# Two attention blocks on one core: K and P transposed in tiles of 64 rows, K no longer by DMA transpose

## The chip, the core and the metric

The kernel runs on one core of one Trainium2 chip. The metric is the device time of one execution in microseconds (us); the median of the runs is quoted. The core has five engines with instruction queues of their own: TensorE (PE, with its weight loads listed apart as PEld), VectorE (DVE), ScalarE (ACT), GpSimd (POOL) and SyncE (SP), which here only starts loads. Transfers go through 16 DMA engines. Matmul results go to PSUM, eight banks of 128 rows by 512 f32 (or 1024 bf16) columns; everything else lies in SBUF.

## The reference

Two independent attention blocks, A and B, with the same shapes; the two results stand side by side in the output.

```python
# x (16, 64, 640), k_cache and v_cache (16, 32, 512, 128), wq (640, 4096), wo (4096, 640), all bf16
q = (x @ wq).reshape(B, Sq, 32, 128).transpose(0, 2, 1, 3)
scores = einsum("bhqd,bhkd->bhqk", q, k_cache) * (128 ** -0.5)
p = softmax(scores, axis=-1)
o = einsum("bhqk,bhkd->bhqd", p, v_cache)
return o.transpose(0, 2, 1, 3).reshape(B, Sq, 4096) @ wo
```

K and V of both blocks are 268 MB, and each byte is used once.

## The kernel before

**Tiling.** Two batches of 64 queries fill the 128 rows: a batch pair `bp`, with batches `j` = 0 and 1. A *step* `g` is one head of a batch pair, a *macro* `m` is two heads, a *chunk* `c` four, and a *group* the 16 heads of one half of the heads. There are 512 steps, 256 macros, 128 chunks and 32 groups: two blocks, two halves of the heads (a block and a half make a *pass*, which keeps its weights), eight batch pairs.

**One macro in order.** K comes from memory with keys on the rows and must be turned so that the head's 128 features are on the rows. KX (`em_KX`, L451) does this on PE: for each batch, eight transposes of 128x128 (L457) put the keys of two heads into bank 7, and KE (L466, DVE) copies the 1024 columns to `ktp_ring`. QP2 (L475, PE) computes q of two heads, ten 128-column matmuls, QE2 (L484, ACT) scales and copies it. SM (L496, PE) makes the scores of one head: two matmuls of 512 columns, one for each batch, on the two column halves of the array (`tile_position=(0, 64 * j)`), so that batch `j` lands in rows 64j to 64j+63 of one of four score banks. MX (L505, DVE) takes the row maxima, EX (L511, ACT) the exponentials and row sums, RC2 (L517, DVE) the reciprocals, NM (L525, POOL) scales P and reorders its columns. TR2 (L534, PE) transposes P of both heads, eight transposes of 128x128 into bank 6; TE2 (L541, DVE) or TA2 (L546, ACT) copies the 1024 columns to `pT_ring`. PV2 (L558, PE) multiplies with V, 16 matmuls of 64 columns with V as the stationary operand; OE2 (L566, ACT) copies it out. OP2 (L574, PE) multiplies with the first 512 columns of wo and adds over the 16 heads of a group in bank 0. Once per group OX (L584, PE) does the same for the last 128 columns, in score bank 0; OVP and OXP (ACT) keep the sums of the first half of the heads, OVF and OXF (DVE) add the second half, and ST (L613) stores from ACT's queue.

**K by DMA.** In the eleven groups of `TGROUPS` (L20) the K of batch 1 is loaded already transposed: LDKT (L651) is one DMA transpose of 2 MB per group into `kd_sb`. There KX and KE run for batch 0 alone, and SM reads `kd_sb`. The x operand comes by DMA transposes too (LDX, L644).

**What orders the work.** `build_plan` writes each engine's program from a template (`PE_T`, `ACT_T`, `DVE_T`, `POOL_T`, L33 to L43): a list of kind, macro offset, which of two heads, and a time in a period of 6.7 us that covers two macros. Each engine executes its list strictly in that order; semaphores make it wait for what it reads and for buffers to come free (`Op.reads`, `Op.writes`). Loads (L195 to L263) all go through SP's queue in one order: a planner sorts them by when they are due, not before the buffer that they fill is free by its own estimate (`SLOT_NS`, `DMA_NS`). K has four slots of a chunk (two DMAs of 512 KB, one for each batch), V five; the last chunk is loaded in halves (`TAIL_SPLIT`).

The transposes of K, and the banks before:

```python
            for t8 in range(8):
                ins = e.transpose(kt_ps[:, t8, :], kn_ring[:, c % NKB, j, hp, t8, :], ident[:, :])
...
        S_BANK0 = 2
        OUT_BANK, QO_BANK, PT_BANK, KT_BANK = 0, 1, 6, 7
```

Of the kernel before, what the change touches and what calls it, by code (L numbers as in the profile page):

```python
# [14 lines left out]
class Cfg:  # L15
    G = 4
    HH = 16
    NKB = 4
    NW = 6
    TGROUPS = (4, 6, 11, 13, 15, 19, 21, 23, 27, 29, 31)  # L20
    TLEAD = 1.0
    NVB = 5
    XLEAD = 1.5
    NQ = 3
    NKT = 5
    NP = 4
    NPN = 4
    NT = 2
    NO = 9
    NR = 8  # L30
    NS = 4
    PERIOD = 6.7
    PE_T = (("SM", 0, 0, 0.0), ("SM", 0, 1, 0.21), ("SM", 1, 0, 0.43), ("SM", 1, 1, 0.64), ("KX", 2, 1, 0.98),  # L33
            ("PV2", -3, 0, 1.43), ("TR2", -2, 0, 1.9), ("OP2", -4, 0, 2.35), ("KX", 3, 1, 2.78), ("QP2", 3, 0, 3.23),
            ("OP2", -3, 0, 3.79), ("OX", -3, 0, 4.2), ("KX", 3, 0, 4.22), ("PV2", -2, 0, 4.67), ("TR2", -1, 0, 5.14),
            ("KX", 4, 0, 5.59), ("QP2", 4, 0, 6.04))
    ACT_T = (("EX", 0, 0, 1.13), ("OE2", -3, 0, 2.1), ("EX", 0, 1, 2.49), ("TA2", -2, 0, 3.15), ("QE2", 3, 0, 4.0),
             ("EX", 1, 0, 4.4), ("OXP", -3, 0, 5.2), ("OE2", -2, 0, 5.34), ("EX", 1, 1, 5.73), ("OVP", -3, 0, 6.4),
             ("QE2", 4, 0, 6.65), ("ST", -3, 0, 6.68))
    DVE_T = (("MX", 0, 0, 0.44), ("MX", 0, 1, 1.06), ("RC2", -1, 0, 1.66), ("KE", 2, 1, 1.68), ("MX", 1, 0, 2.3),  # L40
             ("TE2", -2, 0, 2.6), ("RC2", 0, 0, 3.3), ("KE", 3, 1, 3.43), ("MX", 1, 1, 4.1), ("KE", 3, 0, 4.87),
             ("OXF", -3, 0, 5.3), ("OVF", -3, 0, 5.5), ("TE2", -1, 0, 5.79), ("KE", 4, 0, 6.4))
    POOL_T = (("NM", -1, 0, 1.95), ("NM", -1, 1, 2.8), ("NM", 0, 0, 4.2), ("NM", 0, 1, 5.05))  # L43
    TAIL_SPLIT = 2
    SLOT_NS = 3400.0
    DMA_NS = dict(LDK=3100.0, LDKT=9600.0, LDV=3100.0, LDWQ=3900.0, LDWO=4300.0, LDX=700.0)


class Op:
# [3 lines left out]
    def __init__(self, eng, kind, idx, reads=(), writes=(), dur=0.0, ts=None, aux=None):  # L53
# [12 lines left out]
        self.dma = kind in ("LDK", "LDKT", "LDV", "LDX", "LDWQ", "LDWO", "ST")  # L66


def build_plan(dims, cfg):
# [3 lines left out]
    assert H % HH == 0 and HH % G == 0 and G % 2 == 0 and cfg.NR % 2 == 0 and B % 2 == 0  # L73
# [9 lines left out]
    HG = HH // G  # L83
    MPG = SPB // 2
    MPP = NBP * MPG
    MPC = G // 2
    KT = dims["KT"]

    def step_info(g):
# [8 lines left out]
    def by_dma(m, j=1):  # L98
        return j == 1 and m // MPG in cfg.TGROUPS

# [657 lines left out]
```

## Time and profile before

| | |
|---|---|
| median of 3 runs | 898.91 us (897.99 to 900.96) |
| profiled execution, its own time | 900.23 us |
| its span in the profile | 898.5 us |
| granted TensorE clock | 0.996 of full speed |
| busy: PE, PEld, DVE, ACT, POOL | 857.5, 691.1, 746.6, 628.0, 413.8 us |
| moved by DMA | 296.81 MB, mean 330 GB/s |

The page divides the span among engines and among 40 slices, follows the chain of work that ended last back from the end (here 78% PE and 9% DMA), and lists groups of instructions by line with their number, the mean duration of one and the idle time before them. A matmul's duration includes the way through the array, and consecutive ones overlap: 128 columns show 219 to 221 ns each but follow one another every 56 ns. So the cost of PE's work is read from the distance between starts, which the timeline and the single records give, and not from durations. The same holds, with smaller differences, for DVE and ACT. DMA shares over 1 mean that packets of several transfers lie in a DMA engine at once.

The costliest groups before are, in us of busy time: POOL's scaling of P 413.1 (512 instructions of 843 ns), EX 350.1 (512 of 684), MX 337.3 (512 of 680), KE 290.0 (424 of 684), the transposes of K 263.6 (3392 matmuls), QP2 187.8 (2560), PV2 162.0 (4096), the transposes of P 156.4 (2048). A K or V load of 512 KB takes 9.3 to 9.9 us from issue to landing, a DMA transpose of K 17.9.

### The profile page before, as it was taken

The page shows a single profiled execution, that of the slowest core. Times are in us where ns is not written, and L with a number is a line of the kernel's source. Part 1 is how long each engine was busy: PE and PEld are TensorE (multiplying, and loading weights), DVE is VectorE, ACT ScalarE, POOL GpSimd, SP SyncE. Part 2 cuts the span into 40 slices and gives each one's busy share as a digit, 9 for nine tenths or more (in the row PEclk, how much of TensorE's full clock was granted, in tenths as well). Part 3 has the DMA queues.
Part 4 walks back from the last instruction along what each step waited for, and adds up shares of the span by engine and source line. Part 5 has one row for each costly group of instructions (what it writes and reads, how often), then busy time and mean ns, then how long its engine had stood idle before and what let it go on. Part 6 is the DMA issues. An engine that isn't in the chain of part 4 may idle for free.

```text
span 898.5 us, 33204 instructions
## 1 busy us (share of the span) xinstructions
PE 857.5 (95%) x14016; PEld 691.1 (77%) x14144; DVE 746.6 (83%) x1398; ACT 628.0 (70%) x1651; POOL 413.8 (46%) x518
## 2 busy tenths in 40 slices
PE   4999989999999999999998998999999999999997
PEld 3777777878888877878786787778778777787875
DVE  2888878888888888888887887888888798888896
ACT  1776766777777777767676776777777676776774
POOL 0544444445444454544444444445454444545453
PEclk9999999999999999999999999999999999999999
DMA  9999999999999999999999999999999999999992
GB/s 304 336 340 365 318 272 365 295 361 365 363 366 368 286 361 322 319 369 270 364 361 368 367 260 365 309 324 366 294 363 363 367 370 284 367 286 365 315 333 77
DMA packets 315172, 296.81 MB, mean 330 GB/s; under 512 B 109200, under 2 KB 260752, under 8 KB 315024
## 3 DMA queue, kind: packets, MB, share of 16 engines
q1 hardware_dynamic: 312720, 292.06, 106.3%
q10 hardware_dynamic: 2304, 2.62, 0.9%
q8 instruction: 111, 1.82, 0.9%
q14 instruction: 37, 0.30, 0.1%
HBM read 266.34 MB, written 2.62 MB: 299 GB/s over the span
## 4 chain that ended last, share of the span: by engine, by line
PE 78%; DMA 9%; SPq 7%; DVE 3%; issue 1%; ACT 1%; DVEq 0%; ACTq 0%
PE ps L457 20%; PE ps L475 14%; PE ps L496 12%; PE ps L558 11%; PE ps L534 10%; PE ps L574 9%; DMA kn_ring<-in_B_k_cache_dram 5%; DMA kn_ring<-in_A_k_cache_dram 4%; SPq L651 3%; PE ps L584 3%; SPq L644 2%; DVE ktp_ring L466 1%; SPq L664 1%; DMA wq_sb<-in_A_wq_dram 1%; DVE negmax L505 1%
## 5 line engine op out<-in xcount | busy, mean ns | idle before, releaser
L525 POOL TENSOR_SCALAR pn_ring<-p_ring,recip 128x512 bf16<-128x512 bf16 x512 | 413.1, 843 | 476.1 <-DVE recip L517 475.7
L511 ACT ACTIVATE p_ring<-ps,negmax 128x512 bf16<-128x512 f32 x512 | 350.1, 684 | 100.0 <-DVE negmax L505 100.0
L466 DVE COPY ktp_ring<-ps 128x1024 bf16<-128x1024 bf16 x424 | 290.0, 684 | 82.1 <-PE ps L457 67.2
L505 DVE TENSOR_REDUCE negmax<-ps 128x1 f32<-128x512 f32 x512 | 337.3, 680 | 15.2 <-PE ps L496 4.9
L457 PEld LDWEIGHTS ps<-ident,kn_ring 128*128 128x128 bf16 x3392 | 205.3, 98 | 108.5 <-issue 46.5
L457 PE MATMUL ps<-ident,kn_ring 128*128 128x128 bf16 x3392 | 263.6, 221 | 21.1 <-DMA kn_ring<-in_A_k_cache_dram 11.8
L475 PE MATMUL ps<-xT_sb,wq_sb 128*128 128x128 bf16 x2560 | 187.8, 221 | 1.3 <-DMA wq_sb<-in_A_wq_dram 0.6
L558 PE MATMUL ps<-pT_ring,v_ring 128*128 128x64 bf16 x4096 | 162.0, 193 | 8.6 <-DMA v_ring<-in_B_v_cache_dram 3.1
L475 PEld LDWEIGHTS ps<-xT_sb,wq_sb 128*128 128x128 bf16 x2560 | 154.4, 99 | 16.9 <-ACT oT_ring L566 15.8
L558 PEld LDWEIGHTS ps<-pT_ring,v_ring 128*128 128x128 bf16 x4096 | 141.9, 98 | 28.5 <-issue 26.5
L484 ACT ACTIVATE qT_ring<-ps 128x256 bf16<-128x256 f32 x256 | 98.3, 384 | 86.1 <-PE ps L475 86.0
L534 PE MATMUL ps<-ident,pn_ring 128*128 128x128 bf16 x2048 | 156.4, 219 | 0.0
L566 ACT ACTIVATE oT_ring<-ps 128x256 bf16<-128x256 f32 x256 | 97.6, 381 | 75.3 <-PE ps L558 68.1
L541 DVE COPY pT_ring<-ps 128x1024 bf16<-128x1024 bf16 x174 | 119.5, 687 | 35.5 <-PE ps L534 35.5
L496 PE MATMUL ps<-ktp_ring,qT_ring 128*64 128x512 bf16 x848 | 137.3, 391 | 0.0
L574 PE MATMUL ps<-wo_sb,oT_ring 128*128 128x512 bf16 x384 | 124.5, 379 | 6.8
L534 PEld LDWEIGHTS ps<-ident,pn_ring 128*128 128x128 bf16 x2048 | 118.5, 98 | 0.0
L511 ACT ACTIVATION_READ_ACCUMULATOR p_ring<-ps,negmax 128x1 f32 x512 | 103.1, 201 | 0.0
L546 ACT ACTIVATE pT_ring<-ps 128x1024 bf16<-128x1024 bf16 x82 | 84.0, 1024 | 0.0
L496 PEld LDWEIGHTS ps<-ktp_ring,qT_ring 128*64 128x64 bf16 x848 | 47.1, 110 | 41.0 <-issue 2.1
L517 DVE RECIPROCAL recip<-rowsum 128x2 f32<-128x2 f32 x256 | 40.9, 160 | 14.7 <-ACT p_ring L511 14.6
L496 PE MATMUL ps<-kd_sb,qT_ring 128*64 128x512 bf16 x176 | 47.0, 390 | 0.0
(15 smaller groups left out, 152.0 us busy)
## 6 DMA issues: line engine op xcount, KB each, us to landing
v_ring<-in_A_v_cache_dram SPq DMA_DIRECT2D x128, 512.0 KB, 9.9
v_ring<-in_B_v_cache_dram SPq DMA_DIRECT2D x126, 512.0 KB, 9.8
kn_ring<-in_A_k_cache_dram SPq DMA_DIRECT2D x108, 512.0 KB, 9.4
kn_ring<-in_B_k_cache_dram SPq DMA_DIRECT2D x103, 512.0 KB, 9.3
wq_sb<-in_A_wq_dram SPq DMA_DIRECT2D x8, 640.0 KB, 9.9
wo_sb<-in_A_wo_dram SPq DMA_DIRECT2D x8, 640.0 KB, 10.7
wq_sb<-in_B_wq_dram SPq DMA_DIRECT2D x8, 640.0 KB, 9.7
wo_sb<-in_B_wo_dram SPq DMA_DIRECT2D x8, 640.0 KB, 10.3
```

The costliest lines, as they stand in the source:

```text
L457: ins = e.transpose(kt_ps[:, t8, :], kn_ring[:, c % NKB, j, hp, t8, :], ident[:, :])
L466: ins = e.tensor_copy(dst, src)
L475: ins = e.matmul(q_ps[:, sub * 128:(sub + 1) * 128], wq_sb[:, wslot(ps_, hh // G), kt, (hh % G) * DH:(hh % G + 1) * DH], xT_sb[:, kt, bp * ...
L484: ins = e.activation(qT_ring[:, m % NQ].rearrange("p s q -> p (s q)"), q_ps, ACTF.Copy, scale=scale)
L496: ins = e.matmul(s_bank(2 * m + sub)[64 * j:64 * j + 64, :], qT_ring[:, m % NQ, sub, 64 * j:64 * j + 64], kt, start=True, stop=True, tile_ ...
L505: ins = e.reduce_max(negmax[:, r:r + 1], s_bank(g), axis=AX.X, negate=True)
L511: ins = e.activation(p_ring[:, g % NP, :], s_bank(g), ACTF.Exp, bias=negmax[:, r:r + 1], scale=1.0, accum_out=rowsum[:, r:r + 1])
L525: ins = e.tensor_scalar(dst, src, recip[:, r:r + 1], 1.0, ALU.mult, ALU.mult)
L534: ins = e.transpose(pt_ps[:, sub, t, :], pn_ring[:, g % NPN, t * 128:(t + 1) * 128], ident[:, :])
L541: ins = e.tensor_copy(pT_ring[:, m % NT].rearrange("p s t q -> p (s t q)"), pt_ps_flat)
L558: ins = e.matmul(o_ps[:, col:col + 64], v_ring[:, c % NVB, j, gi, t, :], pT_ring[:, m % NT, sub, t, 64 * j:64 * j + 64], start=(t == 0), s ...
L574: ins = e.matmul(out_ps, oT_ring[:, m % NO, sub, :], wo_sb[:, wslot(ps_, hh // G), hh % G, 0:N0], start=(hh == 0), stop=(hh == SPB - 1))
```

## The change

KX and TR no longer run 128x128 transposes. Each is split into two tiles of 64 rows (`row_transpose`): tile r takes rows 64r to 64r+63 of the operand, uses the row half r of the array (`tile_position=(64 * r, 0)`) and writes 64 columns to a bank of its own. K now has banks 4 and 5, P banks 6 and 7, and the score banks go from four to two. For K the two halves are the two heads of a macro, for P the two batches.

KX handles a whole macro, both batches at once, 32 transposes, and KE copies 2048 columns in one instruction; there are 256 KE where there were 424. TR has 16 transposes per macro, and one of two P copies runs on DVE, the other on ACT. `TGROUPS`, `kd_sb` and LDKT are gone: all of K comes through KX, loaded in 512 KB DMAs that hold two heads of both batches (ten slots). QP4, PV4 and their copies QE4 and OE4 handle a chunk at a time, 512 columns in one bank that q and o share. In the template each half of a turn has one visit for scores, one for KX and TR together, and one for the rest. OX writes to P's first bank instead of score bank 0, all 16 heads at once for the last group too. The last chunk is not split.

The core of the diff (templates, resources, loads, banks, transposes, K's and V's DMAs; the four-head forms of QP, QE, PV and OE differ from the old ones in their loops alone):

```diff
 class Cfg:
     G = 4
     HH = 16
-    NKB = 4
+    NKU = 10
+    NVB = 5
     NW = 6
-    TGROUPS = (4, 6, 11, 13, 15, 19, 21, 23, 27, 29, 31)
-    TLEAD = 1.0
-    NVB = 5
-    XLEAD = 1.5
-    NQ = 3
-    NKT = 5
+    XLEAD = 2.0
+    NQ = 4
+    NKT = 3
     NP = 4
     NPN = 4
-    NT = 2
-    NO = 9
+    NT = 4
+    NO = 10
     NR = 8
-    NS = 4
-    PERIOD = 6.7
-    PE_T = (("SM", 0, 0, 0.0), ("SM", 0, 1, 0.21), ("SM", 1, 0, 0.43), ("SM", 1, 1, 0.64), ("KX", 2, 1, 0.98),
-            ("PV2", -3, 0, 1.43), ("TR2", -2, 0, 1.9), ("OP2", -4, 0, 2.35), ("KX", 3, 1, 2.78), ("QP2", 3, 0, 3.23),
-            ("OP2", -3, 0, 3.79), ("OX", -3, 0, 4.2), ("KX", 3, 0, 4.22), ("PV2", -2, 0, 4.67), ("TR2", -1, 0, 5.14),
-            ("KX", 4, 0, 5.59), ("QP2", 4, 0, 6.04))
-    ACT_T = (("EX", 0, 0, 1.13), ("OE2", -3, 0, 2.1), ("EX", 0, 1, 2.49), ("TA2", -2, 0, 3.15), ("QE2", 3, 0, 4.0),
-             ("EX", 1, 0, 4.4), ("OXP", -3, 0, 5.2), ("OE2", -2, 0, 5.34), ("EX", 1, 1, 5.73), ("OVP", -3, 0, 6.4),
-             ("QE2", 4, 0, 6.65), ("ST", -3, 0, 6.68))
-    DVE_T = (("MX", 0, 0, 0.44), ("MX", 0, 1, 1.06), ("RC2", -1, 0, 1.66), ("KE", 2, 1, 1.68), ("MX", 1, 0, 2.3),
-             ("TE2", -2, 0, 2.6), ("RC2", 0, 0, 3.3), ("KE", 3, 1, 3.43), ("MX", 1, 1, 4.1), ("KE", 3, 0, 4.87),
-             ("OXF", -3, 0, 5.3), ("OVF", -3, 0, 5.5), ("TE2", -1, 0, 5.79), ("KE", 4, 0, 6.4))
-    POOL_T = (("NM", -1, 0, 1.95), ("NM", -1, 1, 2.8), ("NM", 0, 0, 4.2), ("NM", 0, 1, 5.05))
-    TAIL_SPLIT = 2
-    SLOT_NS = 3400.0
-    DMA_NS = dict(LDK=3100.0, LDKT=9600.0, LDV=3100.0, LDWQ=3900.0, LDWO=4300.0, LDX=700.0)
+    NS = 2
+    PERIOD = 5.85
+    PE_T = (("SM", 0, 0, 0.0), ("SM", 0, 1, 0.21), ("KX", 2, 0, 0.54), ("TR", -2, 0, 1.0), ("PV4", -2, 0, 1.35),
+            ("OP", -5, 0, 2.28), ("OX", -5, 0, 2.71), ("SM", 1, 0, 2.82), ("SM", 1, 1, 3.03), ("KX", 3, 0, 3.36),
+            ("TR", -1, 0, 3.82), ("QP4", 2, 0, 4.16), ("OP", -4, 0, 5.28))
+    ACT_T = (("EX", 0, 0, 1.15), ("EX", 0, 1, 1.81), ("OE4", -2, 0, 2.52), ("OVP", -5, 0, 3.0), ("OXP", -5, 0, 3.4),
+             ("EX", 1, 0, 3.97), ("EX", 1, 1, 4.63), ("ST", -5, 0, 4.7), ("TE", -1, 0, 5.3), ("QE4", 2, 0, 6.45))
+    DVE_T = (("MX", 0, 0, 0.44), ("MX", 0, 1, 1.06), ("TE", -2, 0, 1.68, True), ("KE", 2, 0, 1.7),
+             ("TE", -2, 0, 2.85, False), ("OVF", -5, 0, 3.2),
+             ("OXF", -5, 0, 3.4), ("MX", 1, 0, 3.46), ("RC2", 0, 0, 4.08), ("MX", 1, 1, 4.22), ("KE", 3, 0, 4.85),
+             ("RC2", 1, 0, 6.0))
+    POOL_T = (("NM", 0, 0, 4.35), ("NM", 0, 1, 5.2), ("NM", 1, 0, 6.2), ("NM", 1, 1, 7.05))
+    SLOT_NS = 3000.0
+    DMA_NS = dict(LDK=1300.0, LDV=1500.0, LDWQ=1950.0, LDWO=2150.0, LDX=700.0)
...
+        if kind == "KX":
+            return mk(eng, "KX", m, [("kn", m % cfg.NKU), ("ident",)], [("KTB",)], ts)
+        if kind == "KE":
+            return mk(eng, "KE", m, [], [("KTB",), ("ktp", m % cfg.NKT)], ts)
+        if kind == "SM":
+            return mk(eng, "SM", (m, sub), [("qT", m % cfg.NQ), ("ktp", m % cfg.NKT)], [("SB", g % cfg.NS)], ts)
...
+            return mk(eng, "OX", m, [("oT", i % cfg.NO) for i in range(m + 1 - MPG, m + 1)]
+                      + [("wo", wslot(ps_, i)) for i in range(HG)], [("PTB",)], ts)
+        home = {"V": ("OUTB",), "X": ("PTB",)}.get(kind[1])
...
+    by_chunk = ("QP4", "QE4", "PV4", "OE4")
...
+        for k in range(-6, NCHUNK + 6):
+            late = (2 * k - 5) % MPG == MPG - 1
+            for kind, off, sub, t, *when in tmpl:
+                if when and when[0] != late:
+                    continue
...
+        for j in range(2):
+            m = 2 * c + j
+            ready = at["KX", m - cfg.NKU, 0] if m >= cfg.NKU else NEG
+            first = at["KX", m, 0]
+            add(ready, first, first, 2, "LDK", m, [("kn", m % cfg.NKU)], m, cfg.DMA_NS["LDK"])
+            ready = at["PV4", c - cfg.NVB, 0] if c >= cfg.NVB else NEG
+            first = at["PV4", c, 0]
+            add(ready, first, first, 2.5, "LDV", (c, j), [("v", c % cfg.NVB, j)], (c, j), cfg.DMA_NS["LDV"])
     pending = sorted(loads, key=lambda e: (e[1], e[2]))
...
-        kn_ring = sb("kn_ring", [128, NKB, 2, G // 2, 8, DH], BF16)
+        kn_ring = sb("kn_ring", [128, NKU, 2, 8, DH], BF16)
         v_ring = sb("v_ring", [128, NVB, 2, G, 4, DH], BF16)
-        kd_sb = sb("kd_sb", [128, 8, HH * 64], BF16)
-        ktp_ring = sb("ktp_ring", [128, NKT, 2, SK], BF16)
+        ktp_ring = sb("ktp_ring", [128, NKT, 2, 2, SK], BF16)
...
-        S_BANK0 = 2
-        OUT_BANK, QO_BANK, PT_BANK, KT_BANK = 0, 1, 6, 7
+        OUT_BANK, QO_BANK, S_BANK0, KT_BANK, PT_BANK = 0, 1, 2, 4, 6
         out_ps = ps[:, OUT_BANK, :]
-        pt_ps_flat = ps[:, PT_BANK, :].bitcast(BF16)
-        pt_ps = pt_ps_flat.rearrange("p (s t q) -> p s t q", s=2, t=4)
-        q_ps = ps[:, QO_BANK, 0:256]
-        o_ps = ps[:, QO_BANK, 256:512]
-        kt_ps_flat = ps[:, KT_BANK, :].bitcast(BF16)
-        kt_ps = kt_ps_flat.rearrange("p (t s) -> p t s", t=8)
+        qo_ps = ps[:, QO_BANK, :]
+        kt_ps = [ps[:, KT_BANK + r, :].bitcast(BF16) for r in range(2)]
+        kt_ps_both = ps[:, KT_BANK:KT_BANK + 2, :].bitcast(BF16)
+        pt_ps = [ps[:, PT_BANK + r, :].bitcast(BF16) for r in range(2)]
+        pt_ps_both = ps[:, PT_BANK:PT_BANK + 2, 0:256].bitcast(BF16)
+        ox_ps = ps[:, PT_BANK, 0:N1]
 
         def s_bank(g):
             return ps[:, S_BANK0 + g % NS, :]
 
-        ox_ps = ps[:, S_BANK0, 0:N1]
+        def row_transpose(e, banks, r, i, src):
+            half = slice(64 * r, 64 * r + 64)
+            return e.transpose(banks[r][:, 64 * i:64 * i + 64], src, ident[half, half], tile_position=(64 * r, 0))
 
         def em_KX(e, op):
-            m, j = op.idx
-            g0 = 2 * m
-            c, hp = g0 // G, (g0 % G) // 2
             first = last = None
-            for t8 in range(8):
-                ins = e.transpose(kt_ps[:, t8, :], kn_ring[:, c % NKB, j, hp, t8, :], ident[:, :])
-                first = first or ins
-                last = ins
+            for j in range(2):
+                for t in range(8):
+                    for r in range(2):
+                        ins = row_transpose(e, kt_ps, r, 8 * j + t,
+                                            kn_ring[64 * r:64 * r + 64, op.idx % NKU, j, t, :])
+                        first = first or ins
+                        last = ins
             return first, last
 
         def em_KE(e, op):
-            m, j = op.idx
-            src = kt_ps_flat.rearrange("p (t hs pp) -> p t hs pp", t=8, hs=2)
-            dst = ktp_ring[:, kslot(m, j)].rearrange("p hs (t pp) -> p t hs pp", t=8)
-            ins = e.tensor_copy(dst, src)
-            return ins, ins
-
-        def em_QP2(e, op):
-            m = op.idx
+            ins = e.tensor_copy(ktp_ring[:, op.idx % NKT].rearrange("d r j s -> d r (j s)"), kt_ps_both)
+            return ins, ins
+
...
-        def em_TR2(e, op):
+        def em_TR(e, op):
             m = op.idx
             first = last = None
             for sub in range(2):
-                g = 2 * m + sub
                 for t in range(4):
-                    ins = e.transpose(pt_ps[:, sub, t, :], pn_ring[:, g % NPN, t * 128:(t + 1) * 128], ident[:, :])
-                    first = first or ins
-                    last = ins
-            return first, last
-
-        def em_TE2(e, op):
-            m = op.idx
-            ins = e.tensor_copy(pT_ring[:, m % NT].rearrange("p s t q -> p (s t q)"), pt_ps_flat)
-            return ins, ins
-
-        def em_TA2(e, op):
-            m = op.idx
-            ins = e.activation(pT_ring[:, m % NT].rearrange("p s t q -> p (s t q)"), pt_ps_flat, ACTF.Copy)
-            return ins, ins
-
-        def em_PV2(e, op):
-            m = op.idx
-            first = last = None
-            for sub in range(2):
-                g = 2 * m + sub
-                c, gi = g // G, g % G
-                for j in range(2):
-                    for t in range(4):
-                        col = sub * 128 + 64 * j
-                        ins = e.matmul(o_ps[:, col:col + 64], v_ring[:, c % NVB, j, gi, t, :],
-                                       pT_ring[:, m % NT, sub, t, 64 * j:64 * j + 64], start=(t == 0), stop=(t == 3))
+                    for r in range(2):
+                        ins = row_transpose(e, pt_ps, r, 4 * sub + t,
+                                            pn_ring[64 * r:64 * r + 64, (2 * m + sub) % NPN, t * 128:(t + 1) * 128])
                         first = first or ins
                         last = ins
             return first, last
 
-        def em_OE2(e, op):
-            m = op.idx
-            ins = e.activation(oT_ring[:, m % NO].rearrange("p s q -> p (s q)"), o_ps, ACTF.Copy)
-            return ins, ins
-
-        def em_OP2(e, op):
+        def em_TE(e, op):
+            dst = pT_ring[:, op.idx % NT].rearrange("p j s t q -> p j (s t q)")
+            if op.eng == "act":
+                ins = e.activation(dst, pt_ps_both, ACTF.Copy)
+            else:
+                ins = e.tensor_copy(dst, pt_ps_both)
+            return ins, ins
+
...
-        def em_LDKT(e, op):
-            blk, bp, grp, ps_, _ = step_info(2 * op.aux[0])
-            h0 = (ps_ % NHALF) * HH
-            src = blocks[blk][1][2 * bp + 1, h0:h0 + HH].rearrange("h (p t) d -> (h p) (t d)", t=8)
-            ins = e.dma_start_transpose(kd_sb[:, :, :], src)
-            return ins, ins
-
-        def em_LDKV(e, op):
-            c, j, hlo, hhi, _piece = op.aux
+        def em_LDK(e, op):
+            blk, bp, grp, ps_, hh = step_info(2 * op.idx)
+            h0 = (ps_ % NHALF) * HH + hh
+            src = blocks[blk][1][2 * bp:2 * bp + 2, h0:h0 + 2].rearrange("j hs (p t) d -> (hs p) j (t d)", t=8)
+            ins = e.dma_start(kn_ring[:, op.idx % NKU].rearrange("p j t d -> p j (t d)"), src)
+            return ins, ins
+
+        def em_LDV(e, op):
+            c, j = op.aux
             blk, bp, grp, ps_, hh0 = step_info(c * G)
             h0 = (ps_ % NHALF) * HH + hh0
-            if op.kind == "LDV":
-                src = blocks[blk][2][2 * bp + j, h0 + hlo:h0 + hhi].rearrange("g (p t) d -> p g t d", p=128)
-                ins = e.dma_start(v_ring[:, c % NVB, j, hlo:hhi], src)
-            else:
-                src = blocks[blk][1][2 * bp + j, h0 + hlo:h0 + hhi].rearrange("(hp hs) (p t) d -> (hs p) hp t d",
-                                                                              hs=2, t=8)
-                ins = e.dma_start(kn_ring[:, c % NKB, j, hlo // 2:hhi // 2], src)
-            return ins, ins
-
```

## The prediction

> **What bounds the kernel now.** I call a *turn* one pass of the planner's templates: two macros, four heads of one batch pair; there are 128. The page's second part shows the DMA row at 9 tenths in all slices but the last, and PE busy 95%, so either may set the end. I read the busy time by stretches first, cut where the trace shows DMA transposes being issued (columns: stretch, its length, busy us of PE, PEld, DVE, ACT, POOL, granted clock, DMA share, GB/s).
>
> ```profile
> 180.00:295.00 115.00, 114.11 (x1897) 93.01 (x1913) 99.93 (x187) 86.42 (x225) 55.58 (x70) 1.00 1.08 365
> ...
> 643.00:735.00 92.00, 89.76 (x1490) 72.72 (x1501) 78.94 (x149) 66.88 (x177) 42.58 (x53) 1.00 1.08 366
> ...
> 880.00:882.00 2.00, 1.83 (x28) 1.27 (x26) 2.00 (x6) 1.77 (x6) 1.26 (x2) 1.00 0.26 81
> 882.00:898.50 16.50, 11.16 (x179) 7.76 (x180) 8.23 (x16) 6.64 (x19) 6.73 (x9) 0.99 0.03 11
> ```
>
> ```profile
> 112.00:128.00 16.00, 15.84 (x269) 13.05 (x271) 13.60 (x27) 12.32 (x32) 7.12 (x9) 1.00 1.18 239
> ...
> 349.00:368.00 19.00, 18.84 (x309) 15.20 (x310) 16.82 (x34) 13.54 (x36) 8.51 (x11) 1.00 1.20 260
> ...
> 840.00:860.00 20.00, 19.84 (x343) 16.85 (x344) 17.55 (x35) 14.93 (x38) 9.69 (x12) 1.00 1.18 277
> ```
>
> Without a transpose in flight the DMA moves 363 to 366 GB/s whatever the engines do; with one, 239 to 277 at a *higher* DMA share (1.18 to 1.20 against 1.08). The loads end at about 881 us and 17 us of computing follow. The account closes: 296.81 MB at 365 GB/s are 813 us; the eleven stretches with K by DMA last 206 us and move 54.4 MB, worth 149 us, so they lose 57; the first 5 us (91 GB/s) lose 4; the remaining x transposes about 7. Sum 881. **So the memory queue sets the end, and 57 us of it are the price of K by DMA.**
>
> PE is close behind. The chain of waits, in order of time (start, length, line), gives a turn:
>
> ```profile
> 187.99 0.56 PE ps L475 x10
> ...
> 193.83 0.56 PE ps L475 x10
> ...
> 206.42 0.56 PE ps L475 x10
> ...
> 213.15 0.56 PE ps L475 x10
> ```
>
> 5.84 us where half of K comes by DMA, 6.73 where it does not. With 16 OX matmuls (0.90 us in the same chain) per group: 44 x 5.84 + 84 x 6.73 + 32 x 0.90 = 851 us, plus 8.6 before the first transpose and some 12 of tail: 872. The memory floor and PE lie 26 us apart; a change must lower both.
>
> **The terms on PE.** The timeline, start to start, prices PE's visits (columns: start, length, what).
>
> ```profile
> 61.73 1.05 PE L496 MATMUL ps<-ktp_ring,qT_ring 128*64 128x512 bf16 x8
> ...
> 62.72 0.62 PE L457 MATMUL ps<-ident,kn_ring 128*128 128x128 bf16 x8
> ...
> 63.17 0.63 PE L558 MATMUL ps<-pT_ring,v_ring 128*128 128x64 bf16 x16
> ...
> 63.64 0.61 PE L534 MATMUL ps<-ident,pn_ring 128*128 128x128 bf16 x8
> ...
> 65.17 0.69 DVE L466 COPY ktp_ring<-ps 128x1024 bf16<-128x1024 bf16 x1
> ...
> 65.78 0.68 DVE L505 TENSOR_REDUCE negmax<-ps 128x1 f32<-128x512 f32 x1
> ```
>
> Eight 128-column transposes take 0.45 us (56 ns each); sixteen 64-column PV matmuls, each with its own 128x128 weight load, 0.47 (29 ns each); eight score matmuls 0.99. In the records the last score pair is followed by the next mode 312 ns later where the pair itself streams 216, and QP to scores is 149 ns where QP to QP is 56: a change of array mode costs about 95 ns.
>
> The unknown is a 64-row transpose: no row tile runs in this trace. Its 64 columns cost at most a PV matmul, 29 ns, if the two row halves go one after the other, and 14.5 if they go side by side. The nearest row is the score pair, two column halves of the array:
>
> ```profile
> 883.63 0.40 PE L496 MATMUL ps<-ktp_ring,qT_ring 128*64 128x512 bf16 x1
> 883.64 0.40 PE L496 MATMUL ps<-kd_sb,qT_ring 128*64 128x512 bf16 x1
> ...
> 883.87 0.38 PE L496 MATMUL ps<-ktp_ring,qT_ring 128*64 128x512 bf16 x1
> 883.88 0.38 PE L496 MATMUL ps<-kd_sb,qT_ring 128*64 128x512 bf16 x1
> ```
>
> Halves start 4 to 10 ns apart and a pair costs one. Weight loads can follow that fast too: 5% of the gaps between L457's are 15 ns or less. The new emitter gives the halves a bank each, so I take 29 ns a pair. Below that I see no reason to go; the upper end, 58 a pair, is the first rival.
>
> The new turn: transposes of K, 2 x 16 pairs = 0.94 (was 4 x 0.45 = 1.80); of P, 2 x 8 pairs = 0.47 (was 0.90); PV 32 x 29 = 0.94, QP 20 x 56 = 1.12, OP 4 x 216 = 0.86, all as before; scores in two visits, 2 x (0.24 + 0.31) = 1.10; four further changes of mode at 95 ns = 0.38. Sum 5.81; the old turn has 0.12 over its own sum, so 5.93, and OX adds 0.90 / 4: **6.15 us, 128 turns = 788**, with start and tail about 809.
>
> **The other engines per turn.** DVE: a 1024-column copy is 0.61 start to start, as a 512-column f32 reduce is. A 2048-column copy lies between that plus the second half's 0.53 (0.69 less some 0.15 of fixed cost), 1.14, and two old copies, 1.22; I take 1.15. If the wider form fell to the reduce's pace (512 elements in 0.61) it would be 2.4, but same type and source at 1024 columns exclude that. So 4 x 0.61 + 2 x 1.15 + 0.61 + 2 x 0.17 = 5.7, with OVF and OXF 5.8. ACT: 4 x 0.66 + a P copy 0.94 + two 512-column copies at 0.49 (0.28 + 256 more columns) = 4.6. POOL: 4 x 0.79 = 3.2. Two score banks in place of four put SM(1) behind EX(0): MX 1.3 and EX 1.4 after SM(0) stand inside the 2.8 us that the template leaves. OX moves from a score bank to P's pair, where the template copies P ahead of it in that turn; its 0.9 us are in the sum. DVE's in-order queue has KE ahead of MX, so a late K stops maxima too; PE then waits for both at once, which costs nothing while K is what is late.
>
> **The memory queue.** Same bytes, K now in 2 KB pieces. 297 MB at 365: 813. About 13,000 more instructions (PE's 28,160 become some 42,000) are 0.8 MB: 2. First 5 us: 4. The six x transposes stay: between 7 (their 2.6 of 25.7 transposed MB, of 64 us lost) and 12; I take 9. **Loads end near 828, or 6.4 us a turn; PE with 6.15 fits under it.** No ring starves it: ten K and five V slots (five turns) cover 9.9 us from issue to landing.
>
> By the Trainium skill (DMA: Bandwidth & Descriptors, "Where 436 GB/s comes from") a core has about 358 GB/s of its memory. The trace grants 365; by the page this term would be 829 in place of 813.
>
> Tail: the last V loads are due three chunks behind the last K, 6 x 1.43 = 8.6 us. From the last K to the end, by rows: transposes and copy 1.9, two macros of scores, maxima and exponentials to 6, two POOL steps to 8, TR and copy 9.6, PV 10.7, OE4, OP and 16 OX 13.3, final adds 14.4, store 2.4: 17 us, or 8 after the last load. Before had 17, with PE behind, though it loaded its last chunk in halves; unsplit, the last load lands 0.7 later. I take 11.
>
> Span 828 + 11 = 839; the profiled execution lay 1.7 above its span (900.23 against 898.5) and the median 1.3 below that: **840 us**.
>
> **Rivals.**
> 1. *Row halves one after the other* (slower). Each K macro costs 0.94, each P macro 0.47: the turn grows by 1.41 to 7.56, 968 us of turns, 988 in all. It decides from a pair of about 44 ns, where 128 turns and 21 us reach 898. Against it: the score pairs. For it: no row tile in the trace, and 64-column matmuls never stand closer than 27 ns within one tile. By the Trainium skill (TensorE: Matmul & The Clock Gate, "Wait — 56ns, not 53.3ns?") matmuls never start less than about 25 ns apart however few columns; held between tiles, that gives some 50 ns a pair, 7.16 x 128 + 21 = 937 us. The trace's 4 ns between score halves speaks against it.
> 2. *Hand-offs keep PE above the queue's pace.* Six modes a turn, one transpose bank pair, one QO bank for both projections and PV, DVE at 5.8 of 6.4. With 0.5 us of waits a turn, 6.65 x 128 + 21 = 872. For it: DVE's margin is now 10%, was 17%. Against it: the old turn lost only 0.12 to such waits.
> 3. *K in its new shape is read slower*: two batches 4 MB apart per partition. At V's rate by packet time (1 KB in 50.9 ns against 2 KB in 89.7), 134 MB lose some 45 us: 885.
>
> **How the numbers follow.** Forecast 0.70, own range 831 (tail 8, x 7, no price for instructions) to 864 (356 GB/s, the slowest clean stretch, 860 to 880 us). Rival 2: 0.10, 864 to 885. Rival 3: 0.04. Rival 1: 0.14, 905 to 988. Gains that cancel, within 0.3% (what a measurement of this kernel tells from none): 0.02. Faster 0.84. The range 831 to 880 leaves out rival 1, most of rival 3 and edges: about 2 in 10.
>
> **What the profile after would show.** Right: no stretch under 330 GB/s but at x; sixteen K pairs in about 0.47 us with halves under 10 ns apart; PE waits on kn_ring spread over the run; loads ending near 828. Wrong: 32 transposes in 0.9 us, the DMA row under 9, and no kn_ring waits (rival 1); DVE the releaser of L457's and L496's idle time (rival 2); clean stretches under 350 GB/s (rival 3).

## The result, and the profile after

The changed kernel takes **996.36 us** (median of 4 runs, 994.34 to 1007.66) against 898.76 us for the kernel before on the same chip: a ratio of 1.1107, 95% interval 1.1022 to 1.1192 (ratios here are estimated over all executions, so they are not exactly the quotient of the medians). It is 11% slower where 840 us and a gain were forecast. The profiled execution took 996.13 us, with a span of 994.4. Its page, cut to the lines that answer to the first reading of the profile before (busy time, slices, one DMA queue, the chain):

```profile
span 994.4 us, 47021 instructions
PE 841.7 (85%) x20992; PEld 587.6 (59%) x20992; DVE 725.2 (73%) x1184; ACT 638.9 (64%) x1441; POOL 416.4 (42%) x518
...
PEclk9888999989999999999999899999999989999999
DMA  9999998879859999989967999899993999898850
GB/s 284 364 336 366 340 344 289 292 263 348 307 194 367 361 298 309 300 300 319 320 246 255 367 318 337 282 307 308 337 363 128 369 369 333 279 302 285 286 188 15
...
q8 instruction: 166, 2.72, 1.1%
...
PE 82%; issue 13%; SPq 2%; DMA 1%; DVE 1%; ACT 1%; POOL 0%; ACTq 0%
```

PE has less to do than before (841.7 us busy, was 857.5), the DMA moves less in the mean (299 GB/s, was 330), and neither is full any more. The chain holds 13% "issue", time in which the engine waited for nothing that the profile shows; before it was 1%. The same two rows of the page before:

```profile
q8 instruction: 111, 1.82, 0.9%
...
PE 78%; DMA 9%; SPq 7%; DVE 3%; issue 1%; ACT 1%; DVEq 0%; ACTq 0%
```

The waits of PE say where (columns: line, releaser, us in total, times, longest):

```profile
PE ps L401 <- issue: 54.9, 42, 3.2
PE ps L498 <- issue: 39.3, 26, 3.1
PE ps L423 <- issue: 30.1, 17, 2.7
...
PE ps L514 <- issue: 4.9, 5, 2.4
```

Of the releasers that the prediction watched for, kn_ring has no row for PE at all and DVE one of 1.3 us. PE stops in every kind of its work alike, up to 3 us at a time, with no semaphore behind it. One such stop in the timeline, matmuls first, weight loads second (start, length, what, idle before):

```profile
200.27 1.29 PE L423 MATMUL ps<-xT_sb,wq_sb 128*128 128x128 bf16 x20
...
202.48 0.64 PE L401 MATMUL ps<-ident,kn_ring 64*128 64x64 bf16 x32
202.96 0.40 PE L401 MATMUL ps<-ident,pn_ring 64*128 64x64 bf16 x16
203.29 1.11 PE L498 MATMUL ps<-pT_ring,v_ring 128*128 128x64 bf16 x32
...
206.79 1.01 PE L514 MATMUL ps<-wo_sb,oT_ring 128*128 128x512 bf16 x2 [2.40 <-issue]
...
210.13 2.31 PE L423 MATMUL ps<-xT_sb,wq_sb 128*128 128x128 bf16 x20
```

```profile
204.20 0.10 PEld L514 LDWEIGHTS ps<-wo_sb,oT_ring 128*128 128x128 bf16 x1
206.80 0.11 PEld L514 LDWEIGHTS ps<-wo_sb,oT_ring 128*128 128x128 bf16 x1 [2.50 <-issue]
```

Three things stand in these lines. The transposes are as fast as forecast: 32 of K from 202.48 to 202.96, 16 of P to 203.29. Then the weight load of an OP starts at 204.20 and its own matmul only at 206.79. And after the pause the 20 matmuls of L423 take 2.31 us, where they took 1.29 at 200.27: the granted clock has dropped to half, in windows of 3.4 us, 97 us in all (9 us before).

**What PE waits for.** The page lists a DMA queue with the kind "instruction": 166 transfers of 16 KB, 2.72 MB. PE's records (20,992 weight loads, 20,992 matmuls and 655 of its sequencer, such as semaphore waits) number 42,639. That is 64 bytes a record, 256 records a transfer, and 166.6 such blocks (a *block* from here on is one of these, not an attention block). The singled-out stop fits: a transfer of this queue starts at 204.30, lands at 205.27, and PE goes on 1.5 us later. All records can be counted by their place in the program, modulo 256. A stop is here a start that lies more than 0.45 us behind the start before it; matmuls that the trace lacks are filled in from their weight loads; "one place" is record 193 of 256, where 91 of the kernel after's stops lie, give or take four records.

```
                      records  blocks  stops over   us in   at one place  us at     mean
                                of 256   0.45 us     all       mod 256   that place
before                 28,615   111.8       30       38.6           1       0.8     0.84
after                  42,639   166.6      142      192.4          92     150.9     1.64
```

The stops elsewhere are the start and the end of the run, waits for data, and ordinary steps stretched by the half clock. PE stops where one block of 256 instructions ends and the next has not landed; it goes on 1.27 to 1.58 us (in 9 of 10, median 1.41) after the landing. How long after the *preceding* block end the next block lands depends on how busy the DMA engines are in between (kernel after, means; the share counts packet time up to the landing, and over 1 is a backlog):

```
DMA share between         under 0.3  0.3-0.6  0.6-0.8  0.8-0.95  0.95-1.05  over 1.05
block lands after, us          2.2      2.9       3.3       4.1        4.0        5.0
mean stop, us                 0.00     0.24      0.11      0.87       0.99       1.29
blocks                          12        5        13        32         44         59
```

Two stretches of the kernel after show the same in the busy times (stretch, its length, PE, PEld, DVE, ACT, POOL, clock, DMA share, GB/s): 504 matmuls in 25 us beside full loads, 625 beside a third of them.

```profile
300.00:325.00 25.00, 20.79 (x504) 14.36 (x505) 17.34 (x28) 14.68 (x32) 9.29 (x12) 0.93 1.07 369
750.00:775.00 25.00, 22.32 (x625) 15.86 (x623) 21.64 (x35) 18.67 (x44) 11.80 (x15) 1.00 0.41 133
```

So beside full data loads PE gets one block per **6.5 us, 39 instructions a microsecond**: the mean distance of the block ends in the 59 intervals of the last column, 5.0 to the landing and some 1.4 more; its own pace without stops (below) is 4.8 us a block. Between any two block ends exactly one transfer lands (165 of 165 in the kernel after): the supply runs one block ahead and no further, so a slack stretch saves nothing for a dense one.

### The profile page after: what moved, and what is told of

Its sections match the earlier page's. It is cut to its first block, busy times and chain, and to the rows that moved or that the text cites. A ratio compares the mean times of both kernels' runs of the same rounds, so it can differ in the third digit from the quotient of the medians.

```text
span 994.4 us, 47021 instructions
## 1 busy us (share of the span) xinstructions
PE 841.7 (85%) x20992; PEld 587.6 (59%) x20992; DVE 725.2 (73%) x1184; ACT 638.9 (64%) x1441; POOL 416.4 (42%) x518
## 3 DMA queue, kind: packets, MB, share of 16 engines
q8 instruction: 166, 2.72, 1.1%
## 4 chain that ended last, share of the span: by engine, by line
PE 82%; issue 13%; SPq 2%; DMA 1%; DVE 1%; ACT 1%; POOL 0%; ACTq 0%
PE ps L401 22%; PE ps L423 17%; PE ps L439 15%; PE ps L498 14%; PE ps L514 12%; PE ps L524 3%; DMA v_ring<-in_A_v_cache_dram 1%; SPq L591 1%; SPq L584 0%; DVE negmax L448 0%; SPq L570 0%; ACT p_ring L454 0%; ACT pT_ring L486 0%; DVE ktp_ring L415 0%; DVE pT_ring L488 0%
## 5 line engine op out<-in xcount | busy, mean ns | idle before, releaser
L415 DVE COPY ktp_ring<-ps 128x2048 bf16<-128x2048 bf16 x256 | 311.3, 1216 | 30.1 <-PE ps L401 29.5
L401 PEld LDWEIGHTS ps<-ident,kn_ring 64*128 64x128 bf16 x8192 | 140.6, 97 | 145.2 <-issue 142.1
L423 PE MATMUL ps<-xT_sb,wq_sb 128*128 128x128 bf16 x2560 | 182.3, 230 | 38.2 <-issue 30.1
L401 PE MATMUL ps<-ident,kn_ring 64*128 64x64 bf16 x8192 | 174.9, 193 | 31.3 <-issue 29.7
L423 PEld LDWEIGHTS ps<-xT_sb,wq_sb 128*128 128x128 bf16 x2560 | 156.6, 103 | 47.2 <-issue 32.6
L514 PE MATMUL ps<-wo_sb,oT_ring 128*128 128x512 bf16 x512 | 162.3, 400 | 5.2 <-issue 4.9
L486 ACT ACTIVATE pT_ring<-ps 128x1024 bf16<-128x1024 bf16 x128 | 130.6, 1021 | 17.9 <-PE ps L401 17.8
L401 PE MATMUL ps<-ident,pn_ring 64*128 64x64 bf16 x4096 | 108.0, 193 | 29.7 <-issue 25.2
L506 ACT ACTIVATE oT_ring<-ps 128x512 bf16<-128x512 f32 x128 | 76.2, 595 | 63.3 <-PE ps L498 63.0
L432 ACT ACTIVATE qT_ring<-ps 128x512 bf16<-128x512 f32 x128 | 76.9, 601 | 48.2 <-PE ps L423 48.1
L401 PEld LDWEIGHTS ps<-ident,pn_ring 64*128 64x128 bf16 x4096 | 81.4, 97 | 34.0 <-issue 30.6
L514 PEld LDWEIGHTS ps<-wo_sb,oT_ring 128*128 128x128 bf16 x512 | 37.8, 102 | 7.2 <-issue 6.0
```

The costliest lines, as they stand in the source:

```text
L401: return e.transpose(banks[r][:, 64 * i:64 * i + 64], src, ident[half, half], tile_position=(64 * r, 0))
L415: ins = e.tensor_copy(ktp_ring[:, op.idx % NKT].rearrange("d r j s -> d r (j s)"), kt_ps_both)
L423: ins = e.matmul(qo_ps[:, i * 128:(i + 1) * 128], wq_sb[:, wslot(ps_, hh // G), kt, i * DH:(i + 1) * DH], xT_sb[:, kt, bp * 128:(bp + 1) * ...
L432: ins = e.activation(qT_ring[:, s0:s0 + 2].rearrange("p m s q -> p (m s q)"), qo_ps, ACTF.Copy, scale=scale)
L486: ins = e.activation(dst, pt_ps_both, ACTF.Copy)
L514: ins = e.matmul(out_ps, oT_ring[:, m % NO, sub, :], wo_sb[:, wslot(ps_, hh // G), hh % G, 0:N0], start=(hh == 0), stop=(hh == SPB - 1))
```

## The experiments

Theory 1: PE lacks instructions, because the change raised their number by half and the data loads delay their blocks. Theory 2: row tiles, with six changes of array mode a turn, cost this time as such. Theory 3: hand-offs (two score banks, one pair of transpose banks) hold PE up.

**1. The kernel before with more instructions and no row tile.** QP and OP of the kernel before in pieces of 64 columns, each with a weight load of its own.

```diff
-                    ins = e.matmul(q_ps[:, sub * 128:(sub + 1) * 128],
+                for h in range(2):
+                    for kt in range(KT):
+                        lo = sub * 128 + 64 * h
+                        ins = e.matmul(q_ps[:, lo:lo + 64],
...
-                ins = e.matmul(out_ps, oT_ring[:, m % NO, sub, :], wo_sb[:, wslot(ps_, hh // G), hh % G, 0:N0],
+                for n in range(0, N0, 64):
+                    ins = e.matmul(out_ps[:, n:n + 64], oT_ring[:, m % NO, sub, :],
+                                   wo_sb[:, wslot(ps_, hh // G), hh % G, n:n + 64],
```

> The kernel before, with QP2's 128-column matmuls cut into two of 64 and OP2's 512-column matmuls into eight of 64, each with its own weight load: the same sums, no row tile, no new array mode, about 12,300 more PE instructions (28,500 to 40,800, or 111 to 159 blocks of 256), and by the rows of before some 10 to 15 us more PE work. Theory 1 (PE's instructions do not arrive fast enough: one block of 256 per about 6 to 6.5 us while the data loads run): stalls of 1 to 3 us in the middle of a run of matmuls, always 256 PE records apart, a mean clock clearly under 0.99, 950 to 1010 us. Theory 2 (row tiles and their changes of mode cause the waits): no such stalls, 900 to 915 us.

1020.40 us, ratio 1.1345 (1.1292 to 1.1398): above the 950 to 1010 us that were expected. One expected sign failed: the clock stayed at 0.993; these stops are shorter (mean 1.23 us, 1.64 in the kernel after). Its waits of PE (L477 is QP, L561 PV, L578 OP, L457 the transposes of K), and its instruction queue and chain:

```profile
PE ps L477 <- issue: 26.9, 26, 2.0
PE ps L561 <- issue: 20.5, 21, 2.4
PE ps L578 <- issue: 16.1, 18, 2.3
PE ps L457 <- issue: 14.9, 16, 2.0
```

```profile
q8 instruction: 159, 2.61, 1.1%
...
PE 86%; issue 10%; DVE 2%; DMA 1%; ACT 0%; SPq 0%; DVEq 0%; ACTq 0%
```

96 of its 110 stops (118.5 us) lie at one place modulo 256. The stops need neither row tiles nor the new banks: theory 2 loses its ground, and the number of instructions is enough.

**2. The changed kernel with light loads.** PE's program is untouched; K and V loads after the first ten and five carry 16 of 128 rows.

```diff
-            ins = e.dma_start(kn_ring[:, op.idx % NKU].rearrange("p j t d -> p j (t d)"), src)
+            n = 128 if op.idx < NKU else 16
+            ins = e.dma_start(kn_ring[0:n, op.idx % NKU].rearrange("p j t d -> p j (t d)"), src[0:n])
```

> The changed kernel, but after the first ten K and five V slots every K and V load carries 16 of the 128 rows (an eighth of the bytes), so the results are computed from old data; all instructions and waits stay. Theory 1, with the block's way lengthened by the data loads: blocks land about 7 us after the crossing that frees their place instead of 10 to 12, PE needs one per 4.7 us, most stalls go, 805 to 840 us at a clock near 1. Theory 1 with a supply that does not depend on the loads: still 960 to 1000 us. Theory 2 (array modes) or 3 (hand-offs between engines, two score banks): also still 960 to 1000 us, with waits on other engines.

842.63 us, ratio 0.9369 (0.9341 to 0.9397), 3 us above the band of theory 1 and far below the 960 to 1000 us of the others. In the timeline one turn runs from K's transposes to K's transposes two macros on:

```profile
301.64 0.64 PE L401 MATMUL ps<-ident,kn_ring 64*128 64x64 bf16 x32
302.12 0.40 PE L401 MATMUL ps<-ident,pn_ring 64*128 64x64 bf16 x16
302.44 1.11 PE L498 MATMUL ps<-pT_ring,v_ring 128*128 128x64 bf16 x32
...
307.48 0.64 PE L401 MATMUL ps<-ident,kn_ring 64*128 64x64 bf16 x32
```

5.84 us, with all row tiles, modes, banks and hand-offs in place: theories 2 and 3 fall. What is left of stops is 27.8 us, and of half clock 33 us. About half of each lies in the first 100 us, whose loads are whole, and the rest near the weight loads, which stay whole too (stops at 216 to 262, 404 to 460 and 655 to 663 us). Without them PE's own time is 841.3 - 27.8 - 33 / 2 = **797 us**, the figure that the forecast put at 809. With it the kernel after is accounted for: 797 + 151 of stops + 97 / 2 lost to the clock = 996, against a span of 994.4.

**3. The dose of data.** Four versions between these two (each leaves out part of the later K and V bytes). Two load fewer rows (64, 96 in place of 16):

> The changed kernel with K and V loads of 64 of the 128 rows after the first ring fill (half the bytes; results from partly old data). Theory 1: at 150 to 200 GB/s the traces so far show a block landing 3.0 us after the crossing before it and PE going on 1.4 us after that, 4.4 us in all, where PE needs 4.7 per block: nearly as fast as with 16 rows (843 us), 840 to 880 us. If the data loads lengthen the way only when their queues are full: 843 us.

> The changed kernel with K and V loads of 96 of the 128 rows after the first ring fill (three quarters of the bytes). Theory 1: at 250 to 300 GB/s blocks land 4.1 us after the crossing, 5.5 us per block, 167 blocks: 890 to 940 us, between 843 (16 rows) and 996 (128 rows). If the way lengthens only when the queues are full: 843 to 860 us, since PE then takes 6.15 us a turn and the loads only 5.1.

Both missed. The profiled executions took 949.63 and 1047.96 us (a second one of each 964.32 and 1064.78); the version with 96 rows moves 78% of the bytes and is slower than with all of them. The busy time in 100 to 800 us (window, busy us of PE, PEld, DVE, ACT, POOL, clock, DMA share, GB/s), 96 rows:

```profile
100.00:800.00 700.00, 576.72 (x14277) 401.05 (x14274) 491.14 (x800) 436.03 (x984) 282.44 (x348) 0.94 0.94 226
```

226 GB/s fill the DMA engines as 306 do in the kernel after (share 0.92), because a 2 KB packet takes 126 ns here, 134 with 64 rows, and 92 in the kernel after. The dose had been given in bytes where the engines' time counts. So two more, over all 128 rows: half of each row (one of two batches of K, two of four heads of V), and K whole with half of V (the second edit alone).

```diff
+            nj = 2 if op.idx < NKU else 1
+            ins = e.dma_start(kn_ring[:, op.idx % NKU, 0:nj].rearrange("p j t d -> p j (t d)"), src[:, 0:nj])
...
+            ng = G if c < NVB else G // 2
+            ins = e.dma_start(v_ring[:, c % NVB, j, 0:ng], src[:, 0:ng])
```

> The kernel after, with K and V loads that still reach all 128 rows but carry half of each row, from the eleventh K load and the sixth pair of V loads on (the rest of the later K and V bytes is left out, so the output is of old data). The program on PE is that of the kernel after. The loads of 64 and of 96 rows kept the DMA engines busy for 0.77 and 0.94 of the stretch 100 to 800 us, at 176 and 226 GB/s, since a 2 KB packet took 134 and 126 ns there against 92 ns with 128 rows. This one moves about as many bytes as the 64 rows did. Theory 1a (an instruction block waits for what the DMA engines have queued, so their busy share decides): packets at the price of the full loads, a share near 0.5, a few stalls of blocks, 840 to 875 us. Theory 1b (the bytes moved decide): the 957 us of the 64 rows again. Theory 2 (row tiles cost the time as such): near 996.

> The same with the K loads whole and the V loads with half of each row: three quarters of the bytes over all 128 rows (half of the later V bytes is left out). Theory 1a: a busy share near 0.75 and, by the stretches of the kernel after with a share of 0.6 to 0.8 (mean stall of a block 0.2 us) and 0.8 to 0.95 (0.87 us), 30 to 120 us of stalls: 870 to 950 us. Theory 1b: the 1056 us of the 96 rows again, which moved as many bytes. Theory 2: near 996.

856.28 us, ratio 0.9562 (0.9520 to 0.9603), and 911.93 us, ratio 1.0168 (1.0131 to 1.0205): inside both bands of 1a, though the busy shares, expected near 0.5 and 0.75, came out at 0.65 and 0.82. The same view for half of each row:

```profile
100.00:800.00 700.00, 664.57 (x17814) 478.04 (x18032) 617.22 (x1017) 540.54 (x1239) 358.81 (x440) 1.00 0.65 196
```

It moves *more* GB/s than the 64 rows (176) at a lower share (0.65 against 0.77) and is 93 us faster: the bytes don't decide, and the engines' busy time comes nearer. All six with the same PE program, and the account of 797 us + stops at the block ends + half of the time at half clock:

```
kernel                 share  GB/s   stops   half clock   797 + stops + half   span
16 rows                 0.29    73    27.8       33       (gives the 797)      841.3
half of each row        0.65   196    39.7       13              843           849.6
64 rows                 0.77   176   111.5       88              952           947.9
three quarters          0.82   261    82.4       41              900           908.1
after                   0.92   306   150.9       97              996           994.4
96 rows                 0.94   226   193.8      126             1054          1046.2
```

The account closes within 1% each time. The mean share doesn't order 64 rows and three quarters: the stops of the narrow loads are longer (mean 2.07 us against 1.50). What orders them is the backlog. With 64 rows 35 block intervals have a share over 1.05, and blocks land 6.1 us after the preceding block end there; with three quarters they are 26, at 5.1 us (of 165 and 163 intervals). Why narrower loads take longer per packet and delay a block more, no run shows.

**4. Fewer instructions, more streaming.** The changed kernel with K, then P, in 128x128 transposes, and with row tiles for one K macro in four (the copies' views follow; K's edit is shown).

```diff
-                    for r in range(2):
-                        ins = row_transpose(e, kt_ps, r, 8 * j + t, kn_ring[64 * r:64 * r + 64, op.idx % NKU, j, t, :])
+                    ins = e.transpose(kt_ps[j][:, 128 * t:128 * t + 128], kn_ring[:, op.idx % NKU, j, t, :], ident[:, :])
```

> The changed kernel with K by 16 transposes of 128x128 per macro instead of 32 of 64 rows (P stays in row tiles, the copy of 2048 columns stays): 8,192 fewer PE instruction pairs' halves, 34,400 PE records in 135 blocks, but 0.86 us more streaming and two more changes of mode per turn. Theory 1: PE sets the end with 7.2 us a turn, 128 x 7.2 + 21 = 943 us, few stalls, clock at 0.98 or more: faster than the changed kernel although PE has more to do. Theories 2 and 3: slower than the changed kernel, 1020 us or more, or stalls as before.

> The changed kernel with K in 64-row tiles in one macro of four and by 128x128 transposes in the other three: 36,500 PE records in 143 blocks; PE's own turn is 7.2 less a quarter of 1.05 us, 6.95, or 910 us with start and tail. Theory 1 (a block of 256 PE instructions per about 6.4 us at full data rate, less below it): 143 x 6.4 = 915, so both limits meet and the time is 915 to 935 us, some stalls, clock 0.98 or more; a quarter of the row tiles brings some 20 us over the kernel with none for K (947 us), and all of them cost 50. Theory 2 (row tiles as such cost): between 947 and 996 us, about 960.

> The changed kernel with P by eight transposes of 128x128 per macro in place of 16 of 64 rows (K stays in row tiles; the P copies read one bank): 38,500 PE records in 151 blocks, PE's own turn 6.15 + 0.43 = 6.6 us, 863 us in all. Theory 1: 151 blocks at 6.0 to 6.4 us, 910 to 965 us with stalls 256 records apart, so faster than the changed kernel by 3 to 9% though PE streams 55 us more. Theory 2: mode changes are as many as before, so slower than 996 us.

K whole: 947.55 us, ratio 1.0535 (1.0504 to 1.0567), as expected. One in four: 960.51, 1.0692 (1.0654 to 1.0731), missed by 25 to 45 us, and at the "about 960" of theory 2. P whole: 960.14, 1.0688 (1.0633 to 1.0744), in the band of theory 1, where theory 2 had more than 996. The page of the first:

```profile
PE 923.4 (98%) x16896; PEld 668.5 (71%) x16896; DVE 731.0 (77%) x1184; ACT 640.0 (68%) x1441; POOL 416.4 (44%) x518
...
q8 instruction: 134, 2.20, 1.0%
```

PE is busy 82 us longer than in the kernel after, and the kernel is 49 us shorter: at 134 blocks, 7.0 us each, only 7 block ends stop it (5.8 us). The second's time alone can't tell the theories apart; its stops can: 37 of its 58, 42.6 us, lie at the block ends. The expectation missed because it averaged. Its timeline has a whole K macro at 302.33 and a row macro at 305.87:

```profile
302.33 1.07 PE L414 MATMUL ps<-ident,kn_ring 128*128 128x128 bf16 x16
303.33 0.41 PE L401 MATMUL ps<-ident,pn_ring 64*128 64x64 bf16 x16
...
305.87 0.64 PE L401 MATMUL ps<-ident,kn_ring 64*128 64x64 bf16 x32
306.35 0.40 PE L401 MATMUL ps<-ident,pn_ring 64*128 64x64 bf16 x16
```

A row macro takes 0.48 us where a whole one takes 1.00, but its 32 further instructions need 32 / 256 x 6.5 = 0.81 us of supply. The 64 row macros save 64 x 0.52 = 33 us against the first version's span of 945.8, and the stops at the block ends grow from 5.8 to 42.6 us: 949, against a span of 957.7. A mean of 6.7 us a block would have been enough; blocks full of row tiles wait all the same.

**5. Fewer loads in flight.** At most three loads wait in SP's queue, so that a block finds a shorter backlog.

```diff
+                if prog is progs["sp"]:
+                    if len(held) >= cfg.DEPTH:
+                        waits.append(held[-cfg.DEPTH])
+                    held.append((op.sem, op.count))
```

> The changed kernel, but SP lets at most three loads be in flight (it waits for the third last to have landed before it issues the next), so less data is queued ahead of an instruction block; bytes and PE work stay. Theory 1, with the block waiting behind queued data: blocks land sooner, fewer and shorter stalls, 840 to 940 us. Theory 1 with the block slowed by shared engines whatever the queue: 980 to 1005 us. Theories 2 and 3: no change, 990 us or more.

1014.33 us, ratio 1.1269 (1.1199 to 1.1340): missed. Stops near the block ends fell from 150.9 to some 50 us, as theory 1 has it. The mean share between 100 and 800 us is 0.92, as in the kernel after, but only 3 block intervals have a share over 1.05 (59 in the kernel after), and blocks land 3.8 us after the preceding block end in the mean, not 4.2: the queue ahead of a block matters, not the share alone. But three loads move only some 300 GB/s, and PE now waits for data:

```profile
PE ps L499 <- DMA v_ring<-in_B_v_cache_dram: 49.0, 47, 2.6
PE ps L499 <- DMA v_ring<-in_A_v_cache_dram: 46.9, 40, 3.9
```

One loss went and another came; as a test of the total it is inconclusive, and no depth that keeps both was found.

**6. What the kernel before is bound by.** No K by DMA in it, and K by DMA in eight groups in place of eleven.

```diff
-    TGROUPS = (4, 6, 11, 13, 15, 19, 21, 23, 27, 29, 31)
+    TGROUPS = ()
...
+    TGROUPS = (6, 11, 14, 19, 22, 27, 29, 31)
```

> The kernel before with no group's K by DMA transpose: all K through 128x128 transposes. By the prediction's account the loads would end near 828 us and PE, with 128 plain turns of 6.73 us and OX, sets the end: 128 x 6.73 + 29 + 21 = 911 us; 29,900 PE records in 117 blocks, one per 7.8 us, so no stalls for instructions. If K by DMA did not cost the memory queue 57 us, the time would be 935 us or more.

> The kernel before with K by DMA in 8 groups in place of 11. By the same account the loads end 16 us earlier (at 865) and PE has 11 us more (883 with start and tail): 885 to 900 us, 0 to 1.5% faster than before. If PE alone set the end of the kernel before: 908 us or more.

923.69 us, ratio 1.0286 (1.0259 to 1.0313), between the 911 and the 935 us of its two accounts (the chain below speaks for the first), and 893.08 us, ratio 0.9942 (0.9920 to 0.9965), inside the 885 to 900 us expected. The pages' busy lines and chains, none and then eight groups:

```profile
PE 891.7 (97%) x14720; PEld 730.5 (79%) x14848; DVE 775.4 (84%) x1440; ACT 670.0 (73%) x1697; POOL 416.2 (45%) x518
...
PE 94%; DMA 3%; issue 1%; DVE 1%; SPq 1%; ACT 0%; DVEq 0%
```

```profile
PE 861.4 (97%) x14208; PEld 698.9 (78%) x14336; DVE 754.3 (85%) x1410; ACT 638.9 (72%) x1663; POOL 414.6 (47%) x518
...
PE 89%; SPq 3%; DMA 3%; DVE 2%; issue 1%; ACT 1%; DVEq 0%; ACTq 0%
```

With none, PE sets the end (94% of the chain, 78% before). With eight, the chain is PE's at 89%, and the kernel is 0.6% faster than the one before: the fastest full kernel of this study, with 113 blocks of instructions and no row tile.

## Why the prediction was wrong

**The step that failed** is the term "About 13,000 more instructions ... are 0.8 MB: 2 [us]". It priced instructions by their bytes on the data queue. What they need is a supply: 256 at a time, one block ahead, each behind whatever the loads have queued. PE went from 111.8 to 166.6 blocks, and 166.6 blocks at 6.5 us beside full loads are 1083 us, at the 6.0 us that they took in the mean 994. The forecast put both at once, 365 GB/s of data and 42,000 instructions in 840 us (5.0 us a block), which the supply doesn't give. So "PE with 6.15 fits under it" fell too: a turn took 994.4 / 128 = 7.8 us in the mean. With the supply priced at what it cost, the sum would have been PE's 809 + 151 of stops + 49 of half clock = 1009, outside all of the rivals. None of them was this one.

- *What bounds the kernel before*: the memory queue with PE close behind. The eight-group version bears it out from the one side (less K by DMA, 0.6% faster), the version with none from the other (PE sets the end, 2.9% late, though 13 us later than its own account gave).
- *The terms on PE* were right. A pair of row halves in 29 ns: starts in the run at 202.48 us follow after 3 and 35, then 4 and 25 ns, and 32 transposes take 0.48 us (0.47 forecast). The step from row tiles to the next mode is 122 ns between starts, of which 25 are the tiles' own step: 97 for the change (95 forecast). The turn is 5.84 us without OX (5.93 forecast).
- *DVE*: the 2048-column copy takes 1.13 us start to start (1.15 forecast), 1.216 in the records.
- *The memory queue*: slices with full loads move 361 to 369 GB/s (365 used; the 358 cited from the Trainium skill, DMA: Bandwidth & Descriptors, "Where 436 GB/s comes from", lies below them), so rival 3 (K in its new shape read slower) falls; they are short, since PE now paces the loads. "Loads end near 828" failed as a consequence: the last slice but one still moves 188 GB/s.
- *Rival 1* (halves one after the other) falls with the 3 to 5 ns between the two halves. With it the rule cited from the Trainium skill (TensorE: Matmul & The Clock Gate, "Wait — 56ns, not 53.3ns?"), about 25 ns from start to start, doesn't hold between two row tiles here.
- *Rival 2* (hand-offs) falls with the light loads: PE busy 95% and 5.84 us a turn with the same hand-offs.
- *The signs* named two releasers, kn_ring (right) and DVE (rival 2). Neither came. Two of the three signs of rival 1 did, the DMA row under 9 and no kn_ring waits, without its cause: the transposes took 0.48 us, not 0.9. The row that came, "issue" in the middle of a run of one kind of matmul, was on no list; the instruction queue's row was in the page before as well (111 transfers).

## What to carry to other kernels

Beside the streaming time of PE, count its instructions (weight loads and matmuls) and divide by 256: next to a memory queue that is full this chip supplied one such block per 6.5 us, so a kernel of 840 us has room for about 840 / 6.5 = 129 blocks, 33,000 instructions. An edit that trades fewer columns for more instructions pays only while every stretch of 256, not the mean, stays slower than that; here 32 instructions cost 0.81 us of supply and saved 0.52 us. When a profile shows "issue" ahead of every kind of work of an engine, number its records and look for one place modulo 256, and thin the loads without touching the engine's program to confirm it.

## What the runs showed of the hardware

- Instruction blocks wait behind the data that lies in the DMA engines: in the kernel after they landed 2.2 us after the preceding block end under a share of 0.3 and 5.0 us over 1.05, and PE went on 1.4 us after. The Trainium skill (Runtime: NRT & Kernel Launch, "Instruction fetch mechanics") has blocks of 256 instructions, as here, and calls the cost of crossing one "mostly hidden". That holds for the kernel before (one stop of 0.8 us at block ends) and not for the one after (150.9 us).
- A stop of some 2 us can cost twice. Each of the 28 windows of half clock in the kernel after (most 3.4 us, 97 us in all) begins within 1.5 us of the end of a stop of 1.8 us or more; of the 33 stops over 2 us past the first 30 us, 23 are followed by one. The version with K in 128x128 transposes, with few stops, has 7 us.
- Two row tiles of 64 columns start 3 to 5 ns apart; the mean start to start in a run of them is 14.5 ns.
- A load of 96 rows of 128 lasts as long as one of 128 (6.9 us from issue to landing, 7.0 for K in the kernel after), and one of 64 rows 4.8 to 5.0; their 2 KB packets take 126 and 134 ns in the mean in place of 92.
